# Retention and expert layer on one core: a step's transposes in one group, its value and state products in another

## The chip, the cores and the metric

One core of a Trainium2 chip runs the whole kernel. The metric is device time in microseconds from one execution, and the median is taken over several executions. The engines are TensorE (PE, its weight loads PEld), VectorE (DVE), ScalarE (ACT), GpSimd (POOL) and SyncE (SP). Each has a queue of its own that it works off in order, and they wait for each other by semaphores.

## The reference

A retention layer (4 batches, 8 heads, 768 tokens, head size 64) feeds a top-1 layer of 8 experts (3072 tokens of 512, inner size 1024).

```python
for t in range(S):
    state = gamma[None, :, None, None] * state + np.einsum('bhd,bhe->bhde', k[:, :, t], v[:, :, t])
    y[:, :, t] = scale * np.einsum('bhd,bhde->bhe', q[:, :, t], state)
...
logits = x @ w_gate
e_idx = np.argmax(logits, axis=1)
...
eom = 1.0 / (1.0 + np.exp(-(x @ w_output_gate)))
for e in range(E):
    mask = e_idx == e
    h = np.maximum(x[mask] @ w1[e], 0.0)
    ye = h @ w2[e]
    out[mask] = gate_w[mask, None] * eom[mask, e, None] * ye
```

## The kernel before

The kernel has two stages. The first is attention with routing, the second runs the experts one after the other on rows that the first has sorted into DRAM. Expert products are split into high and low halves of fp32 (three products for one), which needs each weight block as `whi` (rounded by ACT, `cast_weights`, L151) and `wlo` (the remainder, by DVE, `low_weights`, L171). Both stages are written with a manual schedule: each engine does its instructions in the order in which the Python code records them, and only the semaphores are placed by the framework. So the order of the calls is the order of the queues.

The attention stage works on pairs of 128-token chunks: 12 pairs `j`, three for each batch (`NJ` = 3, `NPR` = 12). The loop at L715 runs steps `j` = 1 to 10, and each step works on pair `j` while it routes pair `j - 1` and turns pair `j + 1`. In a step PE does:

- `scores(j)` (L349): keys by queries for both chunks, each into a PSUM tile `w` from `wide()` (L306); DVE multiplies them by the causal mask into `am`.
- `inter(j)` (L367): queries by the carried state, into the two PSUM tiles `py`, one for each chunk.
- `logits(j - 1)` (L402) and, after ACT's copy `lt`, one transpose `turn_l` (L413). DVE's `route1` (L426) makes the one-hot choice `oh` and the output logit `z` from it; ACT's `exps` (L447) the sums for the gate.
- `turn_k(j + 1)` (L317) and `turn_q(j + 1)` (L331): eight transposes each into a `w` tile, which ACT copies to `kt` and `qt` (1024 columns each). `turn_q` reads `qr`, made by POOL at the head of the step (`prep_q`, L294).
- `attend(j, c)` (L376): the values `vs` by `am` into `py`, for chunk 0 and 1; DVE's `weigh` (L384) makes `yt` from `py`.
- `state(j, 1)` (L390, not in steps where `j % 3` is 2) and `state(j + 1, 0)`: products of keys and values into the PSUM tile `st`, which ACT copies to `sd`.
- `tokens(j - 1)` (L504): eight transposes of `yt` into a `w` tile, from which ACT writes the gated rows (`rows`, L511, with `gates`, L457, from DVE).
- `counts(j - 1)` (L466): three small bf16 products of `oh`; DVE's `places` (L483) turns them into places, by which POOL's `scatter` (L530) sends rows to DRAM.

PSUM is full: the pool `ps_w` has two `w` tiles of two banks each (L208), handed out in turn, and `ps_1` (L209) has one bank each for the two `py`, `st` and `misc` (logits and counts). A step takes five `w` tiles in the order scores, scores, `turn_k`, `turn_q`, `tokens`, so `tokens` gets the one that `turn_k` had, and each taker waits until the last reader of that tile is done.

`w_at` (L576) names the steps that load the first four weight blocks; the step after each casts them and makes their low halves. SP issues the loads of `q`, `k`, `v` for pair `j + 2` at the head of step `j`.

Of the kernel before, what the change touches and what calls it, by code (L numbers as in the profile page):

```python
# [10 lines left out]
F32 = mybir.dt.float32  # L11
# [21 lines left out]
def retention_moe_kernel(  # L33
# [117 lines left out]
    def cast_weights(s: int):  # L151
        raw = raws.pop(s)
        hi = wpool.tile([P, 2, DM], F32R, name="whi", tag="whi")
        lo = wpool.tile([P, 2, DM], F32R, name="wlo", tag="wlo")

        def perm(t):

            return t[:, 1].rearrange("p (dc a j) -> p a dc j", a=4, j=32)

        r2 = raw[:, 1].rearrange("p (a dc j) -> p a dc j", a=4, j=32)  # L160
        nc.scalar.copy(hi[:, 0], raw[:, 0])  # L161
        nc.scalar.copy(perm(hi), r2)  # L162
        wts[s] = (hi, lo)

        def rest():
            nc.vector.tensor_sub(lo[:, 0], raw[:, 0], hi[:, 0].bitcast(F32))  # L166
            nc.vector.tensor_sub(perm(lo), r2, perm(hi).bitcast(F32))  # L167

        subs[s] = rest

    def low_weights(s: int):  # L171
        subs.pop(s)()

    def split_weights(s: int):
        cast_weights(s)
# [28 lines left out]
    with tc.manual_schedule(engines=None), ExitStack() as actx:  # L204
# [179 lines left out]
        def weigh(j, c):  # L384
            if c == 0:
                yts[j] = ap.tile([P, 2, NG, P], F32, name="yt", tag="yt", bufs=2)
            nc.vector.tensor_tensor(out=yts[j][:, c].rearrange("p g t -> p (g t)"), in0=rt["py"][c],
                                    in1=gq[:, 2 * (j % NJ) + c].rearrange("p g r t -> p (g r t)"), op=ALU.mult)
# [58 lines left out]
        def exps(j):  # L447
            oh, ef, mk, d16, z = rt["r", j]
            ex = sm.tile([P, 2, E], F32, name="ex", tag="ex")
            se = sm.tile([P, 2], F32, name="se", tag="se")  # L450
            ez = sm.tile([P, 2], F32, name="ez", tag="ez")
            for c in range(2):
                nc.scalar.activation(ex[:, c], d16[:, c], AF.Exp, accum_out=se[:, c:c + 1])
            nc.scalar.activation(ez, z, AF.Exp, scale=-1.0)
            rt["e", j] = (se, ez)

        def gates(j):  # L457
            se, ez = rt.pop(("e", j))
# [256 lines left out]
        for j in range(1, NPR - 1):  # L715
# [18 lines left out]
            if j == EARLY + 2:  # L734
                n_late = nc.values_load(late[0:1, 0:1], min_val=0, max_val=1)
                with tc.If(n_late > 0):
                    fill(base0, cnt0, 0, HEAD, sm)
                head_load()
                load_weights(4)
            logits(j - 1)  # L740
            turn_k(j + 1)
            turn_l(j - 1)
            route1(j - 1)
            exps(j - 1)
            attend(j, 0)
            weigh(j, 0)
            if j % NJ < NJ - 1:
                state(j, 1)
            turn_q(j + 1)
            gates(j - 1)  # L750
            for c in {1: (3, 4), 2: (5,)}.get(j, ()):
                more_gq(c, nc.vector)
            if j - 1 in w_at:
                low_weights(w_at[j - 1])
            if j - 2 == PICK:
                choose()
            tokens(j - 1)
            labels(j - 1)
            rows(j - 1)
            counts(j - 1)  # L760
            if j >= 2 and j - 2 != EARLY:
                scatter(j - 2, 1)
            places(j - 1)
            if j - 1 == PICK:
                sort8(cnts, io8, pick)
            if j - 1 == EARLY:
                judge()
            attend(j, 1)
            weigh(j, 1)
            state(j + 1, 0)  # L770
        load_weights(5)

        j = NPR - 1
# [18 lines left out]
        route1(j - 1)  # L792
        run_head(1)
        exps(j - 1)
        gates(j - 1)
        labels(j - 1)
        run_head(12)
# [6 lines left out]
        scatter(j - 1, 0)  # L804
        scatter(j - 1, 1)
        exps(j)
        cast_weights(4)
        run_head(24)
        tokens(j)
# [388 lines left out]
```

## Time and profile before

| | |
|---|---|
| median of 3 runs | 434.25 us (433.07 to 437.07) |
| the profiled execution | 430.92 us |
| its span, first to last instruction | 429.2 us |
| PE busy | 413.0 us, 96% |
| DVE, POOL, ACT busy | 262.7, 190.0, 179.1 us |

The steps of the loop lie between 19 and 116 us of the span, about 9.2 to 9.9 us each; the rest is the last pair, an early part of the first expert, and the experts. In the timelines that follow, a line is a run of like instructions: start in the span, time from the first one's start to the last one's end, engine, source line, operation, output and inputs by name, shape, count, and in brackets the idle time before it with what ended it. A matmul's row holds its run through the array too, so rows overlap, and the pace is read from start to start. For PE `128*64` is rows by columns of the array in use. An fp32 product over part of the array stands in the trace as two instructions, so that the 8 of the program's order are 16 there.

### The profile page before, as it was taken

Reading aid. Unit: us, or ns where it says so; the run is one execution under the profiler, and the core shown is the slowest. Engines: PE = TensorE matmul, PEld = TensorE weight load, DVE = VectorE, ACT = ScalarE, POOL = GpSimd, SP = SyncE. Lnnn points to the kernel's source line nnn. Section 1 sums busy time; section 2 is a strip of 40 time slices with the busy share of each in tenths; the row PEclk is TensorE's granted clock in tenths of the full one; section 3 lists DMA queues with packets and bytes.
Section 4 is the critical chain, followed back from the end, with each engine's and each line's share of the span. In section 5 each row is a group of like instructions: output and inputs, shape, how many; then the busy total and the mean of one; then the engine's idle time right before and its main releaser. Section 6 shows DMA issues by size and latency. Waiting matters only on the chain.

```text
span 429.2 us, 10294 instructions
## 1 busy us (share of the span) xinstructions
PE 413.0 (96%) x3694; PEld 393.4 (92%) x3694; DVE 262.7 (61%) x701; ACT 179.1 (42%) x394; POOL 190.0 (44%) x257
## 2 busy tenths in 40 slices
PE   8999999999999898999999999999999999999990
PEld 5888999999889898899999999999999999999990
DVE  3678677777896748856366556555646656754110
ACT  3244464656446225644335334443534444542110
POOL 7347656566624217350055326506515525523512
PEclk9999999999999999999999999999999999999996
DMA  9999999997464296893394476547539449430102
GB/s 193 209 215 256 246 264 246 258 288 181 150 196 150 70 254 211 246 232 109 99 229 153 124 183 191 150 149 193 174 110 249 143 147 228 154 108 19 44 7 74
DMA packets 126566, 74.06 MB, mean 173 GB/s; under 512 B 56686, under 2 KB 114930, under 8 KB 126504
## 3 DMA queue, kind: packets, MB, share of 16 engines
q1 hardware_dynamic: 119568, 59.30, 55.0%
q0 software_dynamic: 5728, 13.93, 9.3%
q8 instruction: 31, 0.51, 0.5%
q14 instruction: 31, 0.25, 0.2%
q10 hardware_dynamic: 1208, 0.06, 0.2%
HBM read 59.35 MB, written 15.23 MB: 174 GB/s over the span
## 4 chain that ended last, share of the span: by engine, by line
PE 48%; issue 8%; DVE 4%; DMA 3%; POOL 3%; ACT 1%; SPq 1%; POOLq 0%; DVEq 0%; ACTq 0%
PE a L919 24%; PE h L901 24%; POOL out_dram L179 3%; DMA srt<-row,posi 1%; DMA raw<-in_moe_w_dram 1%; DMA xl<-srt 1%; DVE wlo L167 1%; DVE xt L878 1%; DVE wlo L166 1%; ACT xh L879 1%; DVE xw L885 0%; SPq L855 0%; DVE ot L659 0%; DVE hl L906 0%; DVE h L628 0%
## 5 line engine op out<-in xcount | busy, mean ns | idle before, releaser
L179 POOL DMA_INDIRECT out_dram<-ot,idi x84 | 90.8, 1081 | 145.5 <-ACT whi L162 86.3
L901 PE MATMUL h<-xh,whi 128*128 128x224 f32 (+7 forms) x256 | 85.6, 334 | 1.2 <-ACT xh L879 1.2
L919 PE MATMUL a<-hl,whi 128*128 128x224 f32 (+7 forms) x256 | 86.0, 336 | 0.7 <-DVE hl L906 0.6
L901 PE MATMUL h<-xw,whi 128*128 128x224 f32 (+7 forms) x256 | 85.8, 335 | 0.3 <-DVE xw L885 0.2
L919 PE MATMUL a<-hh,wlo 128*128 128x224 f32 (+7 forms) x256 | 85.6, 335 | 0.0
L919 PE MATMUL a<-hh,whi 128*128 128x224 f32 (+7 forms) x256 | 85.6, 334 | 0.0
L901 PE MATMUL h<-xh,wlo 128*128 128x224 f32 (+7 forms) x256 | 85.4, 334 | 0.0
L906 DVE SCALAR_TENSOR_TENSOR hl<-h,hh 128x224 fp32r<-128x224 f32 (+7 forms) x64 | 34.9, 547 | 59.8 <-ACT hh L905 59.7
L905 ACT ACTIVATE hh<-h 128x224 fp32r<-128x224 f32 (+7 forms) x64 | 30.9, 483 | 79.7 <-PE h L901 79.7
L166 DVE TENSOR_TENSOR wlo<-raw,whi 128x512 fp32r<-128x512 f32 x64 | 43.9, 686 | 29.1 <-ACT whi L161 28.9
L161 ACT CAST whi<-raw 128x512 fp32r<-128x512 f32 x64 | 39.6, 619 | 38.5 <-PE a L919 37.1
L901 PEld LDWEIGHTS h<-xh,whi 128*128 128x128 f32 x256 | 48.3, 189 | 1.9 <-ACT xh L879 1.6
L919 PEld LDWEIGHTS a<-hl,whi 128*128 128x128 f32 x256 | 48.2, 188 | 1.6 <-DVE hl L906 1.2
L901 PEld LDWEIGHTS h<-xw,whi 128*128 128x128 f32 x256 | 48.2, 188 | 1.3 <-DVE xw L885 0.9
L919 PEld LDWEIGHTS a<-hh,whi 128*128 128x128 f32 x256 | 48.2, 188 | 0.4
L919 PEld LDWEIGHTS a<-hh,wlo 128*128 128x128 f32 x256 | 48.2, 188 | 0.4
L901 PEld LDWEIGHTS h<-xh,wlo 128*128 128x128 f32 x256 | 48.2, 188 | 0.4
L167 DVE TENSOR_TENSOR wlo<-raw,whi 128x512 fp32r<-128x512 f32 x64 | 43.7, 683 | 0.0
L162 ACT CAST whi<-raw 128x512 fp32r<-128x512 f32 x64 | 39.5, 618 | 0.9 <-DMA raw<-in_moe_w_dram 0.9
L879 ACT CAST xh<-xt 128x416 fp32r<-128x416 f32 (+3 forms) x32 | 16.3, 513 | 41.7 <-DVE xt L878 41.7
L359 DVE TENSOR_TENSOR am<-w,mask 128x1024 f32<-128x1024 f32 x24 | 28.3, 1217 | 5.6 <-PE w L356 5.4
L532 POOL DMA_INDIRECT srt<-row,posi x24 | 24.7, 1030 | 12.3 <-issue 2.8
(178 smaller groups left out, 606.1 us busy)
## 6 DMA issues: line engine op xcount, KB each, us to landing
raw<-in_moe_w_dram SPq DMA_DIRECT2D x128, 256.0 KB, 3.0
qn<-in_q_dram SPq DMA_DIRECT2D x12, 512.0 KB, 6.6
kn<-in_k_dram SPq DMA_DIRECT2D x24, 256.0 KB, 5.8
vn<-in_v_dram SPq DMA_DIRECT2D x24, 256.0 KB, 5.5
xl<-srt SPq DMA_DIRECT2D x12, 211.2 KB, 5.4
xl<-srt SPq DMA_DIRECT2D x12, 195.0 KB, 4.5
out_dram<-ot,idi POOLq DMA_INDIRECT x84, 2.7
xl<-srt SPq DMA_DIRECT2D x8, 113.8 KB, 2.5
```

What stands on the lines that cost most here:

```text
L161: nc.scalar.copy(hi[:, 0], raw[:, 0])
L162: nc.scalar.copy(perm(hi), r2)
L166: nc.vector.tensor_sub(lo[:, 0], raw[:, 0], hi[:, 0].bitcast(F32))
L167: nc.vector.tensor_sub(perm(lo), r2, perm(hi).bitcast(F32))
L179: st = nc.gpsimd.indirect_dma_start(out=dst, out_offset=bass.IndirectOffsetOnAxis(ap=idx, axis=0), in_=src, in_offset=None, bounds_check=n ...
L359: nc.vector.tensor_tensor(out=a.rearrange("p b g t -> p (b g) t"), in0=w.rearrange("p b (g t) -> p (b g) t", g=NG), in1=mask.rearrange("p ...
L532: st = nc.gpsimd.indirect_dma_start(out=srt, out_offset=bass.IndirectOffsetOnAxis(ap=posi[:, c:c + 1], axis=0), in_=row[:, c].rearrange("p ...
L879: nc.scalar.copy(xs[e][0][:, dc, w], tp[:, w])
L901: nc.tensor.matmul(ps[:, 0:C], l[:, 0, w], r[:, dc, 0:C], start=(n == 0), stop=(n == 3 * NDC - 1))
L905: relu = nc.scalar.activation(hh, ps[:, 0:C], AF.Relu)
L906: nc.vector.scalar_tensor_tensor(out=hl, in0=ps[:, 0:C], scalar=0.0, in1=hh.bitcast(F32), op0=ALU.max, op1=ALU.subtract)
L919: mm = nc.tensor.matmul(accs[d][:, 0:C], l[:, 1, w], r, start=(f == 0 and n == 0), stop=(f == NF - 1 and n == 2))
```

## The change

In a step the calls are put in another order: `turn_q` and `tokens` follow `turn_l` at once, then `counts`, `state(j, 1)`, both `attend`s and `state(j + 1, 0)`. In step 1 `counts` and `places` stand behind the second `attend` instead. `exps` is split: the exponential of `z` becomes `shares`, which ACT does behind the copy `qt`. On DVE both `weigh`s stand behind the gates and `places` (in step 1 the first one ahead of `places`). `low_weights` is split by its two subtractions: the first stands ahead of the logits, the second behind `route1`. `sort8` and `judge` move to the end of the step.

```diff
@@ -162,14 +162,17 @@
         nc.scalar.copy(perm(hi), r2)
         wts[s] = (hi, lo)
 
-        def rest():
-            nc.vector.tensor_sub(lo[:, 0], raw[:, 0], hi[:, 0].bitcast(F32))
-            nc.vector.tensor_sub(perm(lo), r2, perm(hi).bitcast(F32))
+        def rest(n):
+            if n == 0:
+                nc.vector.tensor_sub(lo[:, 0], raw[:, 0], hi[:, 0].bitcast(F32))
+            else:
+                nc.vector.tensor_sub(perm(lo), r2, perm(hi).bitcast(F32))
 
         subs[s] = rest
 
-    def low_weights(s: int):
-        subs.pop(s)()
+    def low_weights(s: int, part=None):
+        for n in (0, 1) if part is None else (part,):
+            subs[s](n)
 
     def split_weights(s: int):
         cast_weights(s)
@@ -451,8 +454,10 @@
             ez = sm.tile([P, 2], F32, name="ez", tag="ez")
             for c in range(2):
                 nc.scalar.activation(ex[:, c], d16[:, c], AF.Exp, accum_out=se[:, c:c + 1])
-            nc.scalar.activation(ez, z, AF.Exp, scale=-1.0)
             rt["e", j] = (se, ez)
+
+        def shares(j):
+            nc.scalar.activation(rt["e", j][1], rt["r", j][4], AF.Exp, scale=-1.0)
 
         def gates(j):
             se, ez = rt.pop(("e", j))
@@ -737,37 +742,46 @@
                     fill(base0, cnt0, 0, HEAD, sm)
                 head_load()
                 load_weights(4)
+            low = j - 1 in w_at
+            if low:
+                low_weights(w_at[j - 1], 0)
             logits(j - 1)
             turn_k(j + 1)
             turn_l(j - 1)
             route1(j - 1)
             exps(j - 1)
-            attend(j, 0)
-            weigh(j, 0)
+            turn_q(j + 1)
+            tokens(j - 1)
+            shares(j - 1)
+            labels(j - 1)
+            if j > 1:
+                counts(j - 1)
             if j % NJ < NJ - 1:
                 state(j, 1)
-            turn_q(j + 1)
+            if low:
+                low_weights(w_at[j - 1], 1)
             gates(j - 1)
+            rows(j - 1)
+            if j - 2 == PICK:
+                choose()
+            attend(j, 0)
+            if j > 1:
+                places(j - 1)
+            if j >= 2 and j - 2 != EARLY:
+                scatter(j - 2, 1)
+            weigh(j, 0)
             for c in {1: (3, 4), 2: (5,)}.get(j, ()):
                 more_gq(c, nc.vector)
-            if j - 1 in w_at:
-                low_weights(w_at[j - 1])
-            if j - 2 == PICK:
-                choose()
-            tokens(j - 1)
-            labels(j - 1)
-            rows(j - 1)
-            counts(j - 1)
-            if j >= 2 and j - 2 != EARLY:
-                scatter(j - 2, 1)
-            places(j - 1)
+            attend(j, 1)
+            if j == 1:
+                counts(j - 1)
+                places(j - 1)
+            weigh(j, 1)
+            state(j + 1, 0)
             if j - 1 == PICK:
                 sort8(cnts, io8, pick)
             if j - 1 == EARLY:
                 judge()
-            attend(j, 1)
-            weigh(j, 1)
-            state(j + 1, 0)
         load_weights(5)
 
         j = NPR - 1
@@ -792,6 +806,7 @@
         route1(j - 1)
         run_head(1)
         exps(j - 1)
+        shares(j - 1)
         gates(j - 1)
         labels(j - 1)
         run_head(12)
@@ -804,6 +819,7 @@
         scatter(j - 1, 0)
         scatter(j - 1, 1)
         exps(j)
+        shares(j)
         cast_weights(4)
         run_head(24)
         tokens(j)
```

PE's queue in step 4, before (`w<-ident,kn` is `turn_k`, `misc<-ident,lt` is `turn_l`, `w<-ident,qr` is `turn_q`, `w<-ident,yt` is `tokens`, `py` is `attend`, `st` is `state`, `misc<-oh` begins the counts):

```order
L324 MATMUL w<-ident,kn 128x128 x8
L415 MATMUL misc<-ident,lt 128x128
L380 MATMUL py<-am,vs 64x128 x8
L396 MATMUL st<-vs,kn 64x64 x8
L342 MATMUL w<-ident,qr 128x2x64 x8
L508 MATMUL w<-ident,yt 128x128 x8
L470 LDWEIGHTS tri_b
L470 MATMUL misc<-oh,tri_b 128x16
```

Behind the other counts follow the second `attend` and `state(j + 1, 0)`. The same queue of the changed kernel, same step:

```order
L327 MATMUL w<-ident,kn 128x128 x8
L418 MATMUL misc<-ident,lt 128x128
L345 MATMUL w<-ident,qr 128x2x64 x8
L513 MATMUL w<-ident,yt 128x128 x8
L475 LDWEIGHTS tri_b
L475 MATMUL misc<-oh,tri_b 128x16
L476 LDWEIGHTS ones_b
L476 MATMUL misc<-oh,ones_b 128x8
L477 LDWEIGHTS ones_b
L477 MATMUL misc<-acc,ones_b 128x16
L399 MATMUL st<-vs,kn 64x64 x8
L383 MATMUL py<-am,vs 64x128 x16
```

The first `attend` and the state product have moved from between `turn_l` and `turn_q` to behind the counts; `state(j + 1, 0)` follows as before.

ACT's queue in step 4, before (`kt` and `qt` copy the turned keys and queries, `ex` and `ez` are the exponentials, `row` the gated rows):

```order
L410 COPY lt<-misc 128x128
L328 COPY kt<-w 128x1024
L453 ACTIVATE ex,se<-d_1021 128x8 x2
L454 ACTIVATE ez<-z 128x2
L399 COPY sd<-st 128x256
L346 COPY qt<-w 128x1024
L515 ACTIVATE row<-w,gate 128x4x4x32
```

And in the changed kernel:

```order
L413 COPY lt<-misc 128x128
L331 COPY kt<-w 128x1024
L456 ACTIVATE ex,se<-d_1021 128x8 x2
L349 COPY qt<-w 128x1024
L460 ACTIVATE ez<-z 128x2
L402 COPY sd<-st 128x256
L520 ACTIVATE row<-w,gate 128x4x4x32
```

The copy `qt` has moved ahead of `ez` and `sd`; `lt` and `kt` stand where they stood.

## Rows read from the trace of the kernel before

**Rows 1.** The page: span, busy time of each engine, granted clock in 40 slices.
```profile
span 429.2 us, 10294 instructions
PE 413.0 (96%) x3694; PEld 393.4 (92%) x3694; DVE 262.7 (61%) x701; ACT 179.1 (42%) x394; POOL 190.0 (44%) x257
PEclk9999999999999999999999999999999999999996
```
**Rows 2.** Timeline of PE, step 4 and the start of step 5 (columns ahead).
```profile
start us, us, engine line op out<-in xcount [idle before <-releaser]
...
53.65 0.27 PE L415 MATMUL misc<-ident,lt 128*128 128x128 f32 x1
53.85 1.09 PE L380 MATMUL py<-am,vs 128*64 128x128 f32 x16
54.77 0.63 PE L396 MATMUL st<-vs,kn 128*64 128x64 f32 x16
55.34 1.09 PE L342 MATMUL w<-ident,qr 128*128 128x128 f32 x8
56.27 1.04 PE L508 MATMUL w<-ident,yt 128*128 128x128 f32 x8
57.14 0.17 PE L470 MATMUL misc<-oh,tri_b 128*128 128x16 bf16 x1
...
57.29 1.09 PE L380 MATMUL py<-am,vs 128*64 128x128 f32 x16
58.22 0.63 PE L396 MATMUL st<-vs,kn 128*64 128x64 f32 x16
58.78 2.06 PE L356 MATMUL w<-qt,kt 64*128 64x128 f32 x32
60.77 1.10 PE L373 MATMUL py<-qt,sd 64*64 64x128 f32 x32
61.80 0.65 PE L407 MATMUL misc<-yt,wg 128*32 128x128 f32 x16
```
**Rows 3.** Timeline of ACT, step 4: the copy of the transposed keys.
```profile
53.90 1.01 ACT L328 COPY kt<-w 128x1024 f32<-128x1024 f32 x1 [0.78 <-PE w L324]
```
**Rows 4.** Timeline of all engines, start of step 2: PE and ACT.
```profile
29.54 1.16 PE L356 MATMUL w<-qt,kt 64*128 64x128 f32 x16
29.96 0.85 ACT L518 ACTIVATE row<-w,gate 128x256 f32<-128x256 f32 x2
...
30.86 1.16 PE L356 MATMUL w<-qt,kt 64*128 64x128 f32 x16 [0.16 <-ACT row L518]
...
31.95 1.35 PE L373 MATMUL py<-qt,sd 64*64 64x128 f32 x32
...
33.23 0.64 PE L407 MATMUL misc<-yt,wg 128*32 128x128 f32 x16
```
**Rows 5.** Timeline of PE near the end: transposes behind a wait.
```profile
417.39 1.20 PE L950 MATMUL po<-ident,otl 128*128 128x128 f32 x9 [0.25 <-DVE otl L940]
```
**Rows 6.** Timelines of DVE (steps 4 and 10) and POOL (step 10): route and its disturbance.
```profile
54.42 0.17 DVE L432 TENSOR_TENSOR d<-lg,m 128x16 f32<-128x16 f32 x1
...
55.27 0.20 DVE L439 TENSOR_TENSOR oh<-key,mk 128x16 bf16<-128x16 f32 x1
...
111.63 1.19 DVE L432 TENSOR_TENSOR d<-lg,m 128x16 f32<-128x16 f32 x1
...
110.86 1.91 POOL L290 TENSOR_TENSOR vs<-vn,gv 128x1024 f32<-128x1024 f32 x1
```
**Rows 7.** Timeline of DVE, start of step 2: the last weighing of step 1.
```profile
31.38 0.69 DVE L387 TENSOR_TENSOR yt<-py,gq 128x512 f32<-128x512 f32 x1
```
**Rows 8.** Timeline of PE, step 11.
```profile
117.97 1.32 PE L373 MATMUL py<-qt,sd 64*64 64x128 f32 x32
119.22 0.65 PE L407 MATMUL misc<-yt,wg 128*32 128x128 f32 x16
```
**Rows 9.** Timeline of PE at the start of the program.
```profile
6.24 1.92 PE L342 MATMUL w<-ident,qr 128*128 128x128 f32 x8
```

## The prediction

> **What bounds the kernel now.** I read the page first: TensorE (PE) is busy for 413.0 of 429.2 us, and its clock stands at the top digit in all but the last slice [rows 1]. An engine that is nearly always busy says little about what a new order of its work is worth, so the next view is PE's timeline of one step of the attention stage, and what counts in it is the distance from one start to the next. Step 4 shows no idle time at all, yet equal work takes unequal time [rows 2]. Eight transposes of `tokens` take 57.14 - 56.27 = 0.87 us, 0.109 each; the eight of `turn_q`, which come behind a state product, take 0.93. The single transpose of `turn_l` takes 0.20 where another product follows it. The first `attend` takes 54.77 - 53.85 = 0.92. So PE loses time wherever it goes between transposes over the full array (128*128) and products over half its columns (128*64). The order of PE's queue is the bound of this stage, and only what removes these seams or adds a wait to PE can move the end: what runs behind step 11 starts when PE gets there.
>
> **Part 1: two seams fewer in steps 2 to 10.** Going from `turn_l` to `attend` costs 0.20 - 0.11 = 0.09 ahead of the first product. Inside `attend` another 0.05 goes: sixteen products in seven steps and a half of 0.11 would need 0.87, and they take 0.92. Going back from the state product to `turn_q` costs 0.10 (`attend` to `turn_q`, where no state stands between, shows the same) and 0.06 inside `turn_q` (0.93 against 0.87) [rows 2]. That makes 0.30 us for the pair. In the new order `turn_k`, `turn_l`, `turn_q`, `tokens` and the small counts follow each other, then all products over half the columns; one seam (counts to product) stays as it was. The gain is 9 x 0.30 = 2.7 us. Step 1 gets none: its counts stand behind both `attend`s, so it trades two seams for two others.
>
> **Part 2: a wait that the old order hid.** `tokens` writes the third of the PSUM tiles that `wide()` hands out in turn from two buffers, the one that `turn_k` filled, so it needs ScalarE's copy `kt` to be done. In step 4 that copy starts at 53.90 and takes 1.01, so it ends 54.91 - 53.65 = 1.26 us behind the start of `turn_l` [rows 3]. Before, PE had `attend`, the state product and `turn_q` in between and reached `tokens` 2.62 us behind `turn_l` (56.27 - 53.65) [rows 2]; the copy was never waited for. Now only one transpose and eight more lie between: 0.11 + 0.87 = 0.98 us. PE stands 0.28 us short. It goes on about 0.05 us after ScalarE ends: the one such wait in the trace ended at 30.86, after two activations that span 29.96 to 30.81 [rows 4]. After a stop the second transpose is late too; nine transposes behind a wait span 1.20 us, of which the last takes 0.27, so 0.93 for eight distances against 0.87 without a stop, 0.06 more [rows 5]. The wait costs 0.28 + 0.05 + 0.06 = 0.39 us, in each of ten steps: 3.9 us. From below it would be nothing if `kt` were done 0.28 us sooner; no edit touches that copy or what stands ahead of it, so this end is left to rival (a). From above it is 0.5, if the copy is a tenth slower next to PE's writes. I take 0.39.
>
> **Part 3: what else is moved, and its cover.** The counts need the one-hot `oh` of `route1`. In step 4 it ends at 55.27 + 0.20, 1.82 us behind `turn_l` [rows 6]; counts now stand 0.98 + 0.39 + 0.87 = 2.24 behind it instead of 3.49 [rows 2]. With 0.05 for the signal, 0.37 us of cover is left of 1.62, so I cost this at nothing, but it is the next thing to be late. `shares` moves ScalarE's exponential of `z` behind the copy `qt`, because that copy would otherwise wait for the end of `route1`; the gates come some tenths later by it, and the rows after them are due only when the second `scores` of the next step takes their buffer, now after both `attend`s instead of one. `weigh` for both halves stands late on VectorE, behind `places`; `inter` of the next step, which overwrites what `weigh` reads, comes 1.99 us after that step begins (step 5: 58.78 to 60.77) [rows 2], and that hides it in steps 2 to 10. The low halves of the weights, split in two, run where VectorE waits for the logits and behind `route1`; nothing near waits for them. GpSimd's order doesn't change; its copies for the next step are released by `places`, which now ends a little sooner. No load is moved in SP's queue.
>
> **Part 4: the ends of the stage.** Step 2 waits twice before. Its two groups of scores take 31.95 - 29.54 = 2.41 instead of the 1.99 of step 5, for rows that ScalarE finishes at 30.81; with rows ahead of both `attend`s this 0.42 goes. Its `inter` takes 33.23 - 31.95 = 1.28 instead of 1.03 (60.77 to 61.80), for the last `weigh` of step 1, which begins at 31.38 and takes 0.69 [rows 4, 7]. That `weigh` gets later, because the gates now stand ahead of the first `weigh` and wait for ScalarE's `shares`: by nothing at least, by one `weigh` (0.69) at most, and I take 0.30, an estimate between, nearer the lower end as VectorE does the same operations with one new gap. PE comes to `inter` 0.42 - 0.39 = 0.03 sooner, so this wait grows by about 0.3. In step 11 `inter` takes 119.22 - 117.97 = 1.25 against 1.03 [rows 8]: VectorE is late after step 10, because a subtraction there took 1.19 instead of 0.17 us while GpSimd multiplied from 110.86 to 112.77 [rows 6]. GpSimd runs earlier now, the two should part, and 0.22 goes.
>
> **The sum.** Seams -2.7, ten waits +3.9, step 2 -0.42 + 0.30, step 11 -0.22: +0.86, taken as +0.9 us. The rest of the program, the expert products, begins that much later and is otherwise the same. The profiled execution took 430.92 us, 1.7 more than its span, and lies 3.3 below the median of 434.25 (433.07 to 437.07); its own time would become 431.8. Set on the median, the forecast is 435.1 us.
>
> **A rule that speaks against the change.** Before the clock rose, eight transposes at the start took 1.92 us [rows 9], twice the pace of later ones, so they ran at 1.2 GHz; in the steps they run at 2.4 GHz, and 0.93 + 0.87 = 1.80 us of them in a row (`turn_q`, `tokens`) left the granted clock at its top digit [rows 1, 2]. The Trainium skill, "TensorE: Matmul & The Clock Gate", Part 4 (PE-mode transpose), says that transposes don't count as PE activity in the way products do, and that the full clock doesn't engage for them. By the row the sum stays as it is; by the rule a longer row of transposes could let the clock fall.
>
> **Rivals.**
> (a) *The wait doesn't appear*: the copy is done in time, and only the seams count. For it speaks that ScalarE is idle ahead of the copy; against it that it can't begin before `turn_k` ends, and 1.01 is more than 0.98 less the 0.25 by which it starts behind `turn_l`. Then the sum is -2.7 - 0.42 + 0.30 - 0.22 = -3.0: 431.2 us.
> (b) *The counts wait for `route1`* (slower). VectorE's subtraction took 1.19 instead of 0.17 where GpSimd's multiplication overlapped it [rows 6]; such a meeting makes `oh` 1.0 late, and 0.37 is covered. It decides from a delay of 0.37 on. If GpSimd's new place met it in eight or nine of ten steps, 0.63 x 8.5 = 5.4 us come on top of 0.9: 440.5 us. Against it: in steps 2 to 9 GpSimd multiplies well ahead of `route1`, and it moves further ahead. One meeting, in step 10, would cost 0.6 and lies in the forecast's own range.
> (c) *The clock falls* in the row of 25 transposes: 25 x (1.92 / 8 - 0.109) is 3.3 us a step at most (the 1.92 holds the last one's run-out), 33 us in ten steps: 468 us. The top digit through 1.8 us of transposes in every step speaks against it.
>
> **Chances.** Forecast 0.79, (a) 0.11, (b) 0.07, (c) 0.03. The forecast's own range is 433.0 to 437.5: per step 0.29 to 0.50 for the wait, 0 to 0.69 for step 2, one meeting, and a median that moves by a microsecond or two between runs. The range takes in (a) and leaves (b) and (c) out: 431.2 to 438.0. About 1% (4.3 us) is what a measurement of this kernel can tell from no change. Faster by over 1% needs less than 429.9, below even (a): 0.03. Slower by over 1% is (b) and (c) with a little of it lost to the edge: 0.08. Within 1%: 0.89.
>
> **What would show it.** In PE's timeline of step 4: `turn_l` followed by `turn_q` after 0.11, `turn_q` in 0.87, `tokens` beginning about 1.31 behind `turn_l` with "`kt`" as what ended a wait of some 0.3 us, `counts` at about 2.24, the whole step 0.09 longer. In step 2 no wait for `row`, a longer one for `yt`; in step 11 none. Wrong it would be if `tokens` doesn't wait, if counts come later than 2.3 behind `turn_l`, or if the granted clock leaves its top digit in the steps.

## The result and the profile after

The changed kernel takes 437.09 us (median of 20 executions, 433.29 to 440.65); the kernel before, run beside it, takes 433.06 (20, 432.13 to 437.07). The ratio is 1.006 [1.0038, 1.0083]: within 1%, and slower by more than the measurement's uncertainty. It is smaller than the quotient of the medians because executions that were disturbed are left out of it. The profiled execution took 435.02 us, with a span of 433.3, against 430.92 and 429.2 before [rows 1].

The page of the changed kernel, same lines as of before:

```profile
span 433.3 us, 10298 instructions
...
PE 414.7 (96%) x3694; PEld 393.9 (91%) x3694; DVE 265.2 (61%) x701; ACT 179.4 (41%) x394; POOL 191.3 (44%) x257
...
PEclk9999999999999999899999999999999999999996
```

PE has 1.7 us more of busy time for the same 3694 products and stands 2.4 us longer; one slice in the expert stage has left the top digit. PE's timeline of step 6 (columns as in [rows 2]):

```profile
78.34 2.06 PE L359 MATMUL w<-qt,kt 64*128 64x128 f32 x32
...
81.36 0.65 PE L410 MATMUL misc<-yt,wg 128*32 128x128 f32 x16
81.93 1.09 PE L327 MATMUL w<-ident,kn 128*128 128x128 f32 x8
82.86 0.27 PE L418 MATMUL misc<-ident,lt 128*128 128x128 f32 x1
82.97 1.04 PE L345 MATMUL w<-ident,qr 128*128 128x128 f32 x8
84.18 1.09 PE L513 MATMUL w<-ident,yt 128*128 128x128 f32 x8 [0.18 <-ACT kt L331]
85.11 0.17 PE L475 MATMUL misc<-oh,tri_b 128*128 128x16 bf16 x1
...
85.26 0.69 PE L399 MATMUL st<-vs,kn 128*64 128x64 f32 x16
85.78 1.92 PE L383 MATMUL py<-am,vs 128*64 128x128 f32 x32
87.53 0.64 PE L399 MATMUL st<-vs,kn 128*64 128x64 f32 x16
88.09 2.06 PE L359 MATMUL w<-qt,kt 64*128 64x128 f32 x32
```

Nearly all that was forecast of a step stands here: `turn_q` 0.11 behind `turn_l`, a wait for `kt` ahead of `tokens`, which begins 84.18 - 82.86 = 1.32 behind `turn_l` (forecast 1.31), and counts 85.11 - 82.86 = 2.25 behind it (forecast 2.24). The bracket counts only the time since the modelled end of the transpose before; the cost is the distance from start to start. In step 4, for which the signs were given, `turn_q` comes 0.29 behind `turn_l` and the step is 0.54 longer, for a reason told under e3; `tokens` (1.32) and the counts (2.25) stand as in step 6. Steps 1 to 10 from the start of one step's scores to the next, worked out from PE's timelines (before and changed from the traces of e11 and e9, below, which were taken on one chip in one series of runs):

| step | before | changed | difference | forecast |
|---|---|---|---|---|
| 1 | 10.47 | 10.82 | +0.35 | +0.39 |
| 2 | 9.71 | 9.68 | -0.03 | -0.03 |
| 3 | 9.72 | 9.87 | +0.16 | +0.09 |
| 4 | 9.66 | 10.20 | +0.54 | +0.09 |
| 5, 8 | 9.19 | 9.24 | +0.04 each | +0.09 |
| 6, 7, 9 | 9.64, 9.66, 9.72 | 9.74, 9.76, 9.81 | +0.10 each | +0.09 |
| 10 | 9.79 | 10.27 | +0.48 | +0.09 |
| 11, its `inter` | 1.27 | 1.03 | -0.24 | -0.22 |

Together +1.64 us where +0.86 was forecast. Two terms differ in the first comparison's traces: step 2 of before took 9.87 there, and the changed kernel has another 1.1 us on top, in steps 2 (0.23), 3 (0.18), 6 (0.06) and 10 (0.68), and 2.9 more at 174 to 181 us. In steps 3, 6 and 10 and at 174 us signals come late under GpSimd's scatters, which the trace of before doesn't show; this is told under e1 and e9.

### The profile page after: what moved, and what is told of

The parts are those of the page before. It is cut to its first block, busy times and chain, and to the rows that moved or that the text cites. A ratio compares the mean times of both kernels' runs of the same rounds, so it can differ in the third digit from the quotient of the medians.

```text
span 433.3 us, 10298 instructions
## 1 busy us (share of the span) xinstructions
PE 414.7 (96%) x3694; PEld 393.9 (91%) x3694; DVE 265.2 (61%) x701; ACT 179.4 (41%) x394; POOL 191.3 (44%) x257
## 4 chain that ended last, share of the span: by engine, by line
PE 48%; issue 9%; DMA 4%; DVE 3%; POOL 3%; SPq 1%; ACT 0%; POOLq 0%; DVEq 0%; ACTq 0%
PE h L917 24%; PE a L935 24%; POOL out_dram L182 3%; DMA xl<-srt 3%; DMA srt<-row,posi 1%; SPq L871 1%; DVE xt L894 1%; DVE wlo L167 1%; DVE wlo L169 1%; ACT xh L895 0%; DVE xw L901 0%; DVE h L633 0%; DVE hl L922 0%; POOLq L182 0%; ACT whi L162 0%
## 5 line engine op out<-in xcount | busy, mean ns | idle before, releaser
L182 POOL DMA_INDIRECT out_dram<-ot,idi x84 | 91.8, 1092 | 147.4 <-ACT whi L162 89.2
```

The costliest lines, as they stand in the source:

```text
L182: st = nc.gpsimd.indirect_dma_start(out=dst, out_offset=bass.IndirectOffsetOnAxis(ap=idx, axis=0), in_=src, in_offset=None, bounds_check=n ...
```

## The experiments

Every kernel below computes the whole result. The kernel before took about 433 us in some series of runs and about 429 in others, so each ratio is against the kernel before of its own series. Step lengths are as in the table above.

**e1, the changed kernel again** (no edit, one execution; the kernel before beside it 433.34).

> The changed kernel once more, unaltered, for a second profile. Theory K (ten waits for ScalarE's copy kt, and one meeting of VectorE's moved sort with GpSimd's multiplication) expects tokens again about 1.31 us behind turn_l in eight of ten steps and the sort of step 4 again stretched to about 2 us; these repeat because the order of the queues sets them. Theory S (stalls of PE that the trace gives to no engine: 1.1 us in step 10's inter, 0.4 in step 11's, 1.06 at 176 us with a fall of the clock behind it) expects those three at the same places. If they are chance, they stand elsewhere or not at all, and the span is 1.5 to 3 us shorter than 433.3.

434.28 us, span 432.6. The `kt` waits are nearly the same, and so are the stands in steps 10 and 11. PE's stand at 176 us (1.01 by the bracket, 1.06 in the first trace) was there too, but no fall of the clock behind it. So the extra time in step 10 isn't a chance of one trace. The row behind it, step 10 of the changed kernel, PE, POOL and DVE:

```profile
107.14 2.06 PE L359 MATMUL w<-qt,kt 64*128 64x128 f32 x32
109.12 0.81 PE L376 MATMUL py<-qt,sd 64*64 64x128 f32 x4
110.22 1.00 PE L376 MATMUL py<-qt,sd 64*64 64x128 f32 x26 [0.29 <-issue]
```
```profile
107.40 0.99 POOL L537 DMA_INDIRECT srt<-row,posi  x1 [0.56 <-DVE yt L390]
108.69 0.98 POOL L537 DMA_INDIRECT srt<-row,posi  x1 [0.30 <-issue]
```
```profile
110.34 1.22 DVE L362 TENSOR_TENSOR am<-w,mask 128x1024 f32<-128x1024 f32 x1 [1.79 <-PE w L359]
```

The first group of scores starts at 107.14 and the first half of the 32 products is done by about 108.2, but VectorE gets to multiply it only at 110.34, 0.67 behind the end of the second of two scatters that POOL issues back to back; PE's own `inter` stands in the middle too.

**e2, `kt` copied in two halves**, so that the tile is done sooner:

```
-            if not halved:
+                elif split:
+                    nc.scalar.copy(o[:, c].rearrange(...), x)
+            if not halved and not split:
```

> Changed kernel, with ScalarE copying kt in two halves of 128x512, so that the first half is copied while PE still transposes the second. Theory K: the second half ends 0.9 to 1.0 us behind turn_l instead of 1.26, tokens follow turn_q without a stop at about 0.98, counts come at 1.87 to 1.92 (oh ends 1.82 behind turn_l, no slack left). Each of ten steps loses 0.25 to 0.39 us of its length, 3.0 to 3.3 us in all: about 434 us where the changed kernel has 437.1, that is 0.99 to 1.00 of the kernel before. Theory S (the time went into stalls that belong to no engine, and into the clock): the copy is not what PE lacked, and the time stays within 0.5 us of the changed kernel's, 1.006 of the kernel before.

444.25 us, ratio 1.0263 [1.0231, 1.0294]. A miss with a use: the wait ahead of `tokens` is gone, but a new one stands between the two halves of `turn_k`, since the framework holds the tile as one and lets the second half's transposes wait for the copy of the first, in another bank. PE in step 7 and the row of the groups of waits (total us, times, longest):

```profile
88.43 0.70 PE L327 MATMUL w<-ident,kn 128*128 128x128 f32 x4
89.86 0.66 PE L327 MATMUL w<-ident,kn 128*128 128x128 f32 x4 [0.73 <-ACT kt L331]
```
```profile
PE w L327 <- ACT kt L331: 8.5, 10, 1.3
```

Against the changed kernel the median rose by 444.25 - 437.09 = 7.2 us. Ten stops of PE sum to 8.5, with about 0.1 each for starting again, and ten short ones (3.9 by the forecast) are gone: that makes 5.6. The same trace has two stops for VectorE's `yt` in steps 2 and 3, 2.8 us in all, where the changed kernel has 0.2; what made `yt` late wasn't followed, and the median of the changed kernel holds executions with a lower clock (below), so the sum isn't exact. It does show that waits put into PE's queue in this stage aren't hidden.

**e3, sort back in its place**: `sort8` and `judge` ahead of the weighings, as they stood before.

```
+            if j - 1 == PICK:
+                sort8(cnts, io8, pick)
+            if j - 1 == EARLY:
+                judge()
             weigh(j, 0)
...
             state(j + 1, 0)
-            if j - 1 == PICK:
-                sort8(cnts, io8, pick)
-            if j - 1 == EARLY:
-                judge()
```

> Changed kernel, with sort8 and judge back ahead of the two weighings, where they stood before. Theory K: in step 4 the sort's first operation takes 0.2 instead of 2.05 us, the second masked copy am of that step starts about 1.5 us sooner, turn_k no longer waits 0.38 us for it; the kt waits stay. 0.45 us less than the changed kernel at most, which the time of 436.6 can hardly show; the rows of step 4 show it. Theory S expects the same for step 4, and the three stalls where they were. A theory that the moved sort and judge caused the stall of step 10 as well (judge stands in that step) expects 1.5 us less, with step 10 back at 11.0 us.

436.52 us, 1.0045 [1.0011, 1.0079]. Step 4 went from 10.20 to 9.82; step 10 stayed at 10.96. So the place of the sort is worth 0.4 us, in step 4. VectorE, POOL and PE of the changed kernel there:

```profile
49.44 2.05 DVE L568 SCALAR_TENSOR_TENSOR key<-cnts,io 128x8 f32<-128x8 f32 x1
...
51.88 1.21 DVE L362 TENSOR_TENSOR am<-w,mask 128x1024 f32<-128x1024 f32 x1
```
```profile
49.57 1.89 POOL L293 TENSOR_TENSOR vs<-vn,gv 128x1024 f32<-128x1024 f32 x1
```
```profile
53.15 1.09 PE L327 MATMUL w<-ident,kn 128*128 128x128 f32 x8 [0.38 <-DVE am L362]
```

and the same operation of e3, in its old place:

```profile
48.07 0.16 DVE L568 SCALAR_TENSOR_TENSOR key<-cnts,io 128x8 f32<-128x8 f32 x1
```

An operation on 8 columns takes 2.05 us instead of 0.16: it ends at 51.49, when GpSimd's multiplication beside it ends (51.46); `am` starts late, and `turn_k` waits for the tile that `am` reads. This agrees with the Trainium skill, "SBUF — State Buffer", section "Who interferes with whom", which says that a VectorE instruction with two inputs from SBUF contends with a GpSimd instruction that reads SBUF, and that the shared ports are an exclusive lock. Which of the two took them first can't be read here, since VectorE's row begins 0.13 ahead of GpSimd's.

**e4, both edits** of e2 and e3.

> Both: kt copied in two halves, sort8 and judge ahead of the weighings. Theory K adds the two: 3.0 to 3.8 us less than the changed kernel, 433.5 us, 0.99 to 1.00 of the kernel before; steps 3 to 9 each 0.2 to 0.3 us shorter than before's. Theory S: about the changed kernel's time, or 1 to 1.5 us less if judge is behind the stall of step 10.

446.01 us, 1.0287 [1.0249, 1.0326], with the same ten waits as e2. It shows nothing that e2 and e3 don't.

**e5, the kernel before again** (one execution, another chip; the kernel before 429.01 in this series).

> The kernel before, unaltered, for a second profile. In the changed kernel's traces every signal of TensorE that falls due between the start of a GpSimd indirect DMA issue and about 0.5 us behind its end reaches a waiting engine late: ScalarE's lt starts 0.73 to 1.23 us behind the last product of logits in seven of ten steps instead of 0.34, and in steps 10 and 11, where two such issues stand back to back under scores, am starts 1.1 to 2.0 us late and inter stands 1.1 us. In the one trace of before no signal under such an issue is late (lt 0.34, kt 0.36, am 0.32 each time). Theory G (the hold-up hits whatever signal falls due under an issue, in any kernel) would then expect late signals in this trace too, at those places where issues overlap them (kt in steps 3 to 9, st to sd at the top of steps 3, 4, 5, 8, 10). Theory P (it is a property of the changed program, or of the placement of its data) expects none, as in the first trace, and inter of step 10 in 1.17, of step 11 in 1.25.

429.74 us, span 428.0. No signal is late under any scatter.

**e6, the wait alone taken away**: `kt` in two halves as in e2, with the dependence between the two banks declared void.

```
+                    if first is not None:
+                        tc.declare_no_dep(tr.ins, first, reason="the other bank")
...
+                    cp = nc.scalar.copy(o[:, c].rearrange(...), x)
+                    first = cp.ins
```

> Changed kernel, kt copied in two halves as in the run before, but the transposes of the second half write another bank and no longer wait for the copy of the first. Theory K: the copies of 0.59 each end at about 0.95 us behind turn_l, tokens follow turn_q at 0.98, counts at 1.9; the wait of 0.85 us in turn_k of the run before is gone. Ten steps lose 0.06 to 0.39 us each against the changed kernel, 2.9 to 3.2 us together: 434 us against its 437.1, and 10.3 us less than with the halves that wait (444.3). Where lt is late (steps 6 and 9) turn_l waits as before. Theory G adds: inter in steps 10 and 11 stays 1.1 and 0.5 us too long, as this edit moves nothing on GpSimd. If counts now wait for oh (due 1.87 behind turn_l), the gain per step is 0.05 to 0.2 less.

429.65 us, 1.0016 [0.9982, 1.0049]. Steps 5 to 9 take 8.91, 9.38, 9.39, 8.91, 9.44: each 0.27 to 0.29 less than before, the seams' gain without the wait. The whole lost it again, at three places: step 3 and step 4 are longer than before by 0.25 and 0.36, the first with a wait of PE for `yt` (0.46), the second by the sort, and step 10 takes 10.64 instead of 9.79. There, VectorE, POOL and PE:

```profile
108.45 2.33 DVE L167 TENSOR_TENSOR wlo<-raw,whi 128x512 fp32r<-128x512 f32 x1 [0.21 <-DVEq L747]
```
```profile
108.31 1.90 POOL L293 TENSOR_TENSOR vs<-vn,gv 128x1024 f32<-128x1024 f32 x1
```
```profile
112.23 0.17 PE L481 MATMUL misc<-oh,tri_b 128*128 128x16 bf16 x1 [0.96 <-DVE oh L448]
```

The low half ahead of `route1` is blocked by the same multiplication, `oh` comes late, and the counts wait for it.

**e7, the seam alone put back**: the first `attend` between `turn_q` and `tokens`, where it covers the wait.

```
             turn_q(j + 1)
+            attend(j, 0)
             tokens(j - 1)
...
-            attend(j, 0)
             if j > 1:
                 places(j - 1)
```

> Changed kernel, with the first attend between turn_q and tokens: two changes more between transposes over the full array and products over half of it, and kt is covered again. Theory K with the seam price of the prediction: from turn_q to attend 0.09 and 0.05 inside, from attend to tokens 0.10 and 0.06 inside, 0.30 us; tokens at 2.1 us behind turn_l without a wait, 0.39 saved. Net 0.09 us a step, 0.9 in all: 436.2 us where the changed kernel has 437.1. If the seams cost less than 0.2, the time falls by 2 us or more; if tokens is late anyway, the kt copy was not the releaser. Theory G: lt, inter of step 10 and of step 11 as in the changed kernel.

430.81 us, 1.0042 [1.0027, 1.0057]. Steps 5 to 9 take 9.20, 9.65, 9.66, 9.20, 9.72: those of before to the hundredth. PE in step 6:

```profile
83.26 1.04 PE L345 MATMUL w<-ident,qr 128*128 128x128 f32 x8
84.23 1.09 PE L383 MATMUL py<-am,vs 128*64 128x128 f32 x16
85.25 1.09 PE L513 MATMUL w<-ident,yt 128*128 128x128 f32 x8
86.19 0.17 PE L475 MATMUL misc<-oh,tri_b 128*128 128x16 bf16 x1
```

No wait for `kt`, but the seams are back: `turn_q` takes 0.97 up to the product, the product 1.02. Against the kernel without seam and wait (e10) this is 0.28 us a step. The whole is slower than before because step 4 takes 11.18 instead of 9.66 and step 1 10.73 instead of 10.47. In step 4 it is the sort again: its first operation takes 2.77 us, to 51.86, and GpSimd's multiplication ends at 51.82; `turn_k` waits 1.24 for `am`.

**e8, both scatters of a step back to back** at its head, to make the collision of step 10 in every step.

> Changed kernel, with the two indirect stores of a step issued back to back in steps 2 to 9 too (behind GpSimd's multiplication, where the first one stood; before, the second stood ahead of the next step's scores). Theory G: the pair takes 2.3 us and signals due under it arrive about 0.5 us behind the end of the second: lt starts 1.3 us later than in the changed kernel, turn_l waits for it about 1.0 to 1.3 us in each of steps 3 to 9, 7 to 9 us in all, span 440 to 442. The signals that were late under the moved issue at the top of the steps (st to sd, 0.54 to 0.69) are back at 0.33. Theory P, or that the stalls of steps 10 and 11 have another cause than the pair: no such wait, span within 1.5 us of 433.

430.57 us, span 428.8. In its series no signal was late, and the pairs cost nothing: steps 5 to 9 are those of e9. It doesn't tell the theories apart; it shows only that two issues in a row are not enough by themselves.

**e9, the changed kernel a third time**, on the chip of e1.

> The changed kernel once more, timed. So far its signals were late under GpSimd's indirect stores in three traces, all taken where the kernel before takes 433 us; in the four traces taken where that takes 429 us none was late, whatever the kernel. Theory H (the hold-up belongs to the chip it runs on, not to the program): if the kernel before takes 429 us here, no signal is late, inter of step 10 lies at 1.17, of step 11 at 1.03, kt is waited for in eight steps or more, and the time is 0.9 us above the kernel before by the prediction's sum plus 0.5 for the sort of step 4: 1.002 to 1.004. If the kernel before takes 433 us, signals are late as before and the ratio is 1.006. Theory P (the changed program brings the late signals with it) expects them in both cases.

433.2 us (430.58 to 435.44, four executions), 1.0116 [1.0079, 1.0154] against 428.58. The time is a miss, since 1.002 to 1.004 was expected without late signals. The theory was that late signals belong to the chip or to the program; the same chip and program showed none here, in the one execution that was traced (430.58). The same place of step 6 in both, logits on PE and the copy that waits for them; of e9:

```profile
81.21 0.64 PE L410 MATMUL misc<-yt,wg 128*32 128x128 f32 x16
```
```profile
81.92 0.27 ACT L413 COPY lt<-misc 128x128 f32<-128x128 f32 x1 [2.15 <-PE misc L410]
```

and of the changed kernel in the first comparison, whose logits stand above at 81.36:

```profile
82.48 0.27 ACT L413 COPY lt<-misc 128x128 f32<-128x128 f32 x1 [2.56 <-PE misc L410]
```
```profile
80.91 1.02 POOL L537 DMA_INDIRECT srt<-row,posi  x1 [0.17 <-issue]
```

From logits to copy 1.12 us under an issue of a scatter, 0.71 without the disturbance.

**e10, the wait taken away and the collisions moved**: e6, the sort's place of e3, the second scatter of step 10 behind `prep_v`, and two operations of steps 1 and 2 in other places.

```
             prep_v(j + 1, nc.gpsimd)
+            if j - 2 == EARLY:
+                scatter(j - 2, 1)
...
+            if j == 2:
+                more_gq(5, nc.vector)
             logits(j - 1)
...
                 counts(j - 1)
+            weigh(j, 1)
+            if j == 1:
                 places(j - 1)
-            weigh(j, 1)
```

> Changed kernel with kt in two halves that don't wait for each other; sort8 and judge ahead of the weighings; the gate product for step 2 under the wait for the logits; in step 1 the last weighing ahead of places; in step 10 the second indirect store behind GpSimd's products, so that these end 1.3 us sooner and leave VectorE's route alone. Theory K: steps 3 to 10 each 0.28 us shorter than before's, step 2 and 3 without the waits for yt (0.3 and 0.5), step 4 without the 0.5 of the sort, counts of step 10 no longer waiting 1.2 for oh. Against the kernel before: -0.28 x 9 and -0.4 in step 2 and -0.2 in step 11, about -3 us, 0.993 (0.990 to 0.997). If VectorE's and GpSimd's new meetings eat it (theory M, every move on these two engines makes another), the ratio lies at 0.998 to 1.003, as with the two halves alone (1.0016).

426.82 us (12 executions, 425.7 to 428.5), 0.9954 [0.9936, 0.9973]: faster than before by 0.5%, and than the changed kernel. Steps 3 to 10: 9.44, 9.39, 8.91, 9.37, 9.38, 8.91, 9.45, 9.52. PE in step 6, and ACT's two copies:

```profile
80.94 0.27 PE L424 MATMUL misc<-ident,lt 128*128 128x128 f32 x1
81.05 1.04 PE L351 MATMUL w<-ident,qr 128*128 128x128 f32 x8
81.93 1.06 PE L519 MATMUL w<-ident,yt 128*128 128x128 f32 x8
82.82 0.17 PE L481 MATMUL misc<-oh,tri_b 128*128 128x16 bf16 x1
```
```profile
80.76 1.07 ACT L334 COPY kt<-w 128x512 f32<-128x512 f32 x2 [0.35 <-PE w L328]
```

`tokens` begins 0.99 behind `turn_l` (forecast for rival (a): 0.98). The move in step 2 was a bad one: that operation now lasts 1.46 us beside GpSimd's multiplication, and the counts of step 2 wait 0.60.

**e11, the kernel before a third time** (one execution, beside e9 and e10).

> The kernel before, a third profile, on the chip of the two runs above. Theory H: its signals are late exactly if those of the changed kernel are late in the same call. If they are, the kernel before pays too: lt of its steps falls just ahead of the store's issue and stays at 0.34, st to sd in steps 3, 4, 5, 8 and 10 and kt in steps 3 to 9 lie under an issue and come 0.3 to 0.6 late; most of that is off TensorE's path, so its span grows less than the changed kernel's. Theory P: none of its signals is late, whatever those of the changed kernel do.

430.55 us, span 428.8, no late signals. It is the column "before" of the table.

**e12, e10 with `kt` copied whole**: only the wait is given back.

> The tuned kernel with kt copied as one piece again, all else as in it. Theory K: the ten waits of tokens are back, 0.29 us in eight steps, 0.06 and 0.12 where lt is late anyway, with 0.06 each for the restart: 2.9 us. The tuned kernel stood at 0.9954 of the kernel before, so this one at 1.002 (1.000 to 1.005), its steps 5 to 9 0.3 to 0.37 us longer than the tuned one's (9.39, 8.91, 9.37, 9.38, 8.91). Theory M (the meetings of VectorE and GpSimd that the tuning took away were the whole gain, the wait costs nothing by itself since it is made up elsewhere): 0.995 to 0.998, the steps as long as the tuned one's. Where signals are late under the indirect stores (kernel before at 433 us), both come 0.1 to 0.3 per cent higher, by the stores in steps 10 and 11.

430.08 us (12 executions), 1.002 [1.000, 1.004]. Its steps 3 to 10 are 0.33 to 0.38 longer than those of e10, 2.9 together, and PE waits for `kt` again in each (`tokens` 1.27 to 1.32 behind `turn_l`); in step 6:

```profile
82.70 0.27 PE L424 MATMUL misc<-ident,lt 128*128 128x128 f32 x1
...
84.02 1.09 PE L519 MATMUL w<-ident,yt 128*128 128x128 f32 x8 [0.18 <-ACT kt L337]
```

The ratios of the two, each against the kernel before of its own series, differ by 0.66% or 2.8 us, and their intervals don't meet. So the wait, with nothing else edited, costs about that. Steps 1 and 2 differ by more (0.40 and 0.72), but there a wait for `qr` and a longer one for `oh` (1.13 against 0.60) come in, and e12 had reached step 1 0.80 earlier.

## Why the prediction was right or wrong

**The verdict and the mechanism of the steps were right; the time was 2 us low, and a lucky error kept it from being 3.** 437.09 was measured for 435.1 forecast, inside the range of 431.2 to 438.0. By the ratio the change costs 0.006 x 433.06 = 2.6 us (1.6 to 3.6), by the medians 4.0, where 0.9 was forecast. The forecast was set on 434.25, 1.2 above the 433.06 that the kernel before took beside the changed one; that error hides 1.2 of a miss of 3.1.

**Part 1, the seams: right.** 0.30 a pair was forecast; between e7, which has them, and e10, which has neither seam nor wait, steps 5 to 9 differ by 0.28 to 0.29.

**Part 2, the wait: right.** 0.39 a step was forecast; between e12 and e10 it is 0.33 (steps 5 and 8) to 0.38. The kernel gives back for the wait a little more than it gets for the seams, as the sum said. e2 and e6 show from both sides that it isn't hidden: with longer waits in the same ten steps the kernel is 7.2 us slower, and without any wait steps 5 to 9 keep the seams' 0.27 to 0.29.

**Part 3, what costs nothing: wrong at two places.** "The low halves of the weights ... nothing near waits for them" holds where they are not blocked. In step 10 of e9 the half ahead of `route1` took 2.06 us beside GpSimd's multiplication, `oh` was late, and the counts came 2.63 behind `turn_l`, past the 2.3 that the forecast named as a sign of being wrong. VectorE, POOL and PE:

```profile
110.77 2.06 DVE L167 TENSOR_TENSOR wlo<-raw,whi 128x512 fp32r<-128x512 f32 x1 [0.21 <-DVEq L741]
```
```profile
110.37 1.90 POOL L293 TENSOR_TENSOR vs<-vn,gv 128x1024 f32<-128x1024 f32 x1
```
```profile
114.28 0.17 PE L475 MATMUL misc<-oh,tri_b 128*128 128x16 bf16 x1 [0.21 <-DVE oh L442]
```

In the first comparison's trace the two didn't meet, since a late `am` held VectorE up there, and the counts stand at 2.25:

```profile
112.91 0.69 DVE L167 TENSOR_TENSOR wlo<-raw,whi 128x512 fp32r<-128x512 f32 x1 [0.21 <-DVEq L741]
```

So this costs 0.39 in e9 and nothing there, where the late signal costs more. The meeting of e9 is the mechanism of rival (b), at the one place where the forecast's own range had it (0.6), by another operation than the one named. The step that failed in Part 3 was to look for meetings only among the operations of `route1`. The other place, the sort ahead of the masking (`am`) of step 4, in both traces, wasn't costed at all: +0.45 above the forecast for that step, of which e3 gives back 0.4. Above the forecast these two are 0.45 + 0.39 = 0.84 us in the table, and the sum was too small by 1.64 - 0.86 = 0.78; the rest cancels. And Part 4's "GpSimd runs earlier now, the two should part" is right for the subtraction that it spoke of (step 11's `inter` is back at 1.03), wrong for step 10 as a whole, where GpSimd met the low half instead.

**Part 4, steps 2 and 11: right in sum, partly by luck.** In e9 `inter` of step 2 takes 1.42 (1.28 before), so its wait grew by 0.14 and not 0.30; the step's -0.03 comes out because the wait for `row` that goes was 0.26 in e11 and not 0.42. In the first comparison's traces `inter` grew by 0.37, to 1.65. Step 11's -0.22 was -0.24: its `inter` starts at 119.25 in e9 and the logits at 120.28, and before it took 1.25 [rows 8].

**"The rest of the program ... is otherwise the same": wrong.** This is the step of the forecast behind most of the missing microseconds, and it goes both ways. At about 168 to 172 us PE waits for `xh`: 1.20 in e11, 0.81 in e9, 0.50 in e10. e9 had come to the first expert product 1.5 behind e11, and behind this wait it stood 0.1 ahead. The shorter wait is 0.39 of that; two more stops, for `hl` (0.15 and 0.38), are in e11 and not in e9; why they are missing wasn't followed. The two profiled executions took 430.58 and 430.55, so the table's +1.64 is not in the time of the one execution that it was read from. The changed kernel of the first comparison went the other way. Its PE, POOL and then the stretches (columns: stretch, length, busy time of PE, PEld, DVE, ACT, POOL, granted clock, DMA share, GB/s):

```profile
174.30 0.47 PE L917 MATMUL h<-xh,whi 128*128 128x436 f32 x1 [1.20 <-ACT xh L895]
...
176.70 0.33 PE L935 MATMUL a<-hh,whi 128*128 128x224 f32 x1 [1.06 <-issue]
```
```profile
173.35 0.98 POOL L182 DMA_INDIRECT out_dram<-ot,idx  x1 [0.30 <-issue]
174.64 1.12 POOL L182 DMA_INDIRECT out_dram<-ot,idx  x1 [0.31 <-issue]
```
```profile
173.00:176.00 3.00, 1.25 (x4) 0.67 (x4) 2.37 (x5) 1.61 (x3) 2.15 (x3) 1.00 0.82 253
176.00:179.00 3.00, 2.30 (x11) 2.28 (x11) 1.73 (x5) 1.82 (x4) 0.00 (x0) 0.62 0.67 227
179.00:182.00 3.00, 3.00 (x14) 2.86 (x14) 1.88 (x4) 1.14 (x2) 0.00 (x0) 0.81 0.55 176
```

A wait for `xh`, then a stand of 1.06 behind two scatters; PE does 1.25 us of work in three, and then the granted clock falls to the lower level, 1.2 GHz, from 176.75 to about 180.2 us (0.62 and 0.81 are means of stretches that hold only part of it). Against the first trace of before the changed kernel is 2.1 us behind at 165 us and 4.9 from 181 on, 4.1 at the end. Of the 2.9 that it loses there the stand is 1.25, as in e1, which had it and kept its clock; so the fall costs about 1.6. A stand alone doesn't bring it.

Of the 17 executions of the changed kernel that the ratio counts, the ten at a mean granted clock of 0.988 to 0.993 have a median of 434.2 and the seven at 0.984 to 0.987 one of 438.3; of the kernel before, 17 executions beside e1 to e4, three were at the lower clock, and the other 14 have a median of 432.9. So at the higher clock the two kernels lie about 1.2 us apart, near the forecast's 0.9, and the executions at the lower clock are likely the larger part of what the forecast missed (one trace shows where the clock falls, and it is of the upper ten; the other executions show only their mean). Of all executions whose clock is on record, of any kernel, those at 0.987 or less lie in the series in which the kernel before takes 433 us. Why the changed kernel, whose expert stage is the same code, is at the lower clock more often stays open: that its offset and the late signals bring scatters and PE's waits together at 174 us was argued from one trace, not shown.

e9 holds a second open point: its profiled execution took 430.58, the other three 433.2 to 435.4 at clocks of 0.988 to 0.992, and no trace was taken of one of those. By its median the change costs 4.6 us there, of which the steps explain 1.6.

**The trace under the forecast.** It took 430.92 and holds no late signal, and beside the changed kernel the kernel before took 433.06. Its signals in such a series were never traced; that they are late there as well is likely from e1 to e4 but not shown.

**The rivals.** (a) is what e10 makes: without the wait steps 5 to 9 gain 0.27 to 0.29, where (a) said 0.30. (b) came in one step of ten in e9, and in none in the first comparison's trace. (c) had its premise right and its outcome wrong. The first transposes do run at the lower level: they follow each other after 0.21 us, later ones after 0.11, and the pace changes where the trace's records of the granted clock begin, at 11.66 us before and 9.50 in the changed kernel. (A page's digits ahead of that have no record behind them, so the first slice's top digit [rows 1] isn't a measurement.) In e1 the records begin at 8.86, within `turn_k`, whose eight take 1.63 where the eight ahead of them take 1.92; PE had done nothing but transposes since 5.95:

```profile
5.95 1.92 PE L345 MATMUL w<-ident,qr 128*128 128x128 f32 x8
7.66 1.63 PE L327 MATMUL w<-ident,kn 128*128 128x128 f32 x8
```

And with 25 transposes in a row in each step the granted clock stays at 1.00 (changed kernel, columns as above):

```profile
60.00:100.00 40.00, 39.45 (x678) 35.86 (x676) 29.94 (x114) 21.44 (x56) 26.00 (x41) 1.00 1.04 262
```

So the rule weighed ahead, of the Trainium skill's "TensorE: Matmul & The Clock Gate", Part 4, isn't borne out by these traces: the clock rose in a row of transposes, didn't fall behind them, and where it fell, PE had stood.

## What to carry to other kernels

When work is regrouped in a queue, count for each buffer how much work stood between its fill and its reuse: here the group saved 0.28 us of seams and uncovered 0.33 to 0.38 of a copy that had lain beside other work, and a copy that ends sooner (two halves in two banks, with the framework told that they are apart) took the wait away. That alone left the time as before (e6); with the collisions on VectorE and GpSimd moved as well it paid (e10). When an operation with two inputs from SBUF is moved on VectorE, look at what GpSimd does at the new place, for every operation that moves, small ones too: 8 columns took 2 us. And a stage that follows isn't a constant: its own waits and clock gave back 1.6 us in one trace and added 2.9 in another, so two traces of one kernel are worth taking before an offset is carried to the end.

## What the runs showed that was not expected

**Late signals under scatters.** In the series of the first comparison and of e1 to e4 (before at 433 us), a signal from PE that falls due while POOL issues an indirect store, or up to about 0.5 us behind that, reaches the engine that waits for it 0.3 to 0.7 us behind the issue's end (the copy `lt` of step 3 in the first comparison came 0.4 late within the issue); two issues 0.3 apart act as one. In the series of e5 to e12 (before at 428.6 to 429.0) none is late under the same issues. The chip of e1 is that of e9, so it isn't the chip, and e1 and e9 are one program. What sets it for a series stays open. The two kinds of series lie about 4 us of 430 apart for the kernel before, more than e10 gains; how much of that is late signals isn't shown, since the kernel before wasn't traced in a series at 433. Only the comparison within a series is safe from it.

**The dependence of a whole tile.** A transpose into the second bank of a PSUM tile waited for a copy out of the first (e2); with the dependence declared void it didn't (e6).
